# Attention followed by an MLP: more layer-norm rows transposed by transfers, token rows loaded one head earlier

## The chip, the cores and the metric

The kernel runs on one core of one Trainium2 chip. The metric is device time in microseconds: the median of several executions. Five engines work side by side: TensorE (PE: matmuls and its own transposes), VectorE (DVE), ScalarE (ACT), GpSimd (POOL) and SyncE (SP), which only issues transfers here. Each engine runs its instructions in the order in which the program issues them; waits between engines go through semaphores.

## The reference

For 8 batches of 8 heads, 576 tokens and head width 64, causal attention with a bias from a running sum of `s`, then a layer norm and a two-matrix MLP with a residual:

```python
scores = (q @ k.T) / 8                        # per batch and head, 576 x 576
cum    = cumsum(max(s, 0))                    # along the tokens
scores = where(causal, -1e9, scores + min(-(cum[:, None] - cum[None, :]), 0))
attn   = softmax(scores) @ v                  # 576 x 64
x      = heads side by side                   # 576 x 512 per batch
xn     = (x - mean) / sqrt(var + 1e-6) * g_ln
out    = x + max(xn @ w_ch1, 0) @ w_ch2       # 512 -> 2048 -> 512
```

## The kernel before

**Heads and units.** The 64 (batch, head) pairs are numbered n = 8b + h. The first batch and a half are written out step by step (`PLAN`); from n = 18 on a loop issues, for each n: `pre(n)`, the scores of head n, MLP units, `post(n)`, more units, and the attention-times-v of head n - 2 (`pv_next`). A *unit* is a quarter of an MLP tile: four 512-column matmuls on PE, either of the first matrix (`mlp1`, line 537, tile `ph`) or of the second (`mlp2`, line 555, tile `py`). A batch has 32 units in `queue`, and they fill PE between the attention steps. Line 983 sets the head (`end`) by whose close one batch's units are used up and the next batch's are queued: n = 19 for batch 0's, then 8i + 3 for i up to `NXD` = 6 and 8i + 4 above. `nu` is the number of units still given to a head after two fixed ones.

**Keys and queries.** Four heads make a group `gam` (16 groups, two a batch). Groups 0 to 4 are brought in by other means. From group 5 on, token rows are loaded in float32 by SP (`ld_rows`, line 175, tile `rowtmp`, five tiles of at most 128 tokens, two transfers each, a pool of six buffers), cast to bf16 by POOL into `rows[t]` with the bias columns beside them (`cast_rows`, lines 192 and 195), and transposed into `kq[home(gam)]` by a transposing transfer that SP issues (`tr_rows`, line 208). `rows` lies in the storage of `kq[2]`, which group 2 has used before; there is one `rows[t]` for each t, so a cast waits until the group before has been transposed, and two `kq` homes alternate. With m = n - 4 gam, `pre` loads tiles 0 and 1 at m = -6, 2 and 3 at -5, 4 at -4; `post` casts them one head later each, and transposes 0 and 1 at m = -4 and the rest at -3. The scores of the group start at m = 0. At n = 14 `pre` clears the unused columns of `rows` (line 855).

**Layer norm.** When a batch's attention is complete, DVE makes the normalised tiles `xn` (`ln_xn`, line 499): four tiles for an even batch, five for an odd one (the fifth holds the last 64 tokens of two batches). Each must be transposed into `xT` (or `xTm`) before `mlp1` reads it. Up to `NXD` the loop has PE transpose it (`ln_tr`, line 526, four 128 x 128 transposes a tile) and DVE or ACT copy it out of PSUM (line 116); for the last two batches SP issues a transposing transfer instead (`ln_tr_dma`, line 518). In the loop at batch b it is batch b - 1's rows that are normalised, at h = 1; the PE transposes follow at h = 2 and 3. In the transfer branch tiles 0 to 2 are normalised and sent at h = 1 and tiles 3 and 4 at h = 2, with a unit after each.

**What shares a queue.** SP issues, in program order: the row loads, the row transposes, the `xn` transfers and the stores of `out`. POOL issues the loads of v, of the weights and of the first pairs, and also runs the casts and the causal masking of the exponentials (`affine_select`, lines 366 and 396).

Of the kernel before, what the change touches and what calls it, by code (L numbers as in the profile page):

```python
# [9 lines left out]
F32 = mybir.dt.float32  # L10
# [5 lines left out]
P = 128  # L16
# [3 lines left out]
def kernel(  # L20
# [11 lines left out]
    nc = tc.nc  # L32
    B, H, S, D = q.shape
# [5 lines left out]
    NF = S // P  # L39
    NT = NF + 1  # L40
    TL = S - NF * P
    SP = NT * P
    BH = B * H
    KA = D + 4
    OB, OC, OD = 512, 1024, 1536
    EW = 1664
    G = 4
    NG = BH // G
    NPE = 5
    NM = 10  # L50
    NHW = 16
    NXD = 6
    KT = 96
    QT = 6
    QP = S // QT
# [31 lines left out]
    kq = [const.tile([P, 2, G, SP], BF16, name=f"kq{i}") for i in range(3)]  # L87


    def home(gam):  # L90
        return 2 if gam == 2 else gam % 2


    spare = kq[2].rearrange("p u h s -> p (u h s)")
    rows = [
        spare[:, i * 2 * G * P : (i + 1) * 2 * G * P].rearrange(
            "p (u h c) -> p u h c", u=2, h=G
        )
        for i in range(NT)
    ]  # L100
# [58 lines left out]
    def ld_cast_pair(g):  # L159
        ld_cast("k", g)  # L160
        ld_cast("q", g)

    def ld_cast_v(b, t):
        pn = P if t < NF else TL
        nc.gpsimd.dma_start(  # L165
            out=v_bf[b % 2][:pn, t, :, 0:D],
            in_=v[b, :, t * P : t * P + pn, :].rearrange("h s d -> s h d"),
        )

    def ld_rows(gam, t):  # L170
        pn = P if t < NF else TL
        b, h0 = gam // 2, (gam % 2) * G
        tmp = stage.tile([P, 2, G, D], F32, name="rowtmp", tag="st")
        for u, src in enumerate((k, q)):
            nc.sync.dma_start(  # L175
                out=tmp[0:pn, u],
                in_=src[b, h0 : h0 + G, t * P : t * P + pn, :].rearrange("h s d -> s h d"),
            )
        loaded["rows", gam, t] = tmp

    def ld_cast_rows(gam, t):
        pn = P if t < NF else TL
        b, h0 = gam // 2, (gam % 2) * G
        for u, src in enumerate((k, q)):
            nc.gpsimd.dma_start(
                out=rows[t][0:pn, u, :, 0:D],
                in_=src[b, h0 : h0 + G, t * P : t * P + pn, :].rearrange("h s d -> s h d"),
            )
# [10 lines left out]
    def bias_of_rows(gam, t):  # L199
        pn = P if t < NF else TL  # L200
        nc.vector.tensor_copy(
            out=rows[t][0:pn, :, :, D:KA], in_=cT[0:pn, t, :, gam * G : (gam + 1) * G, :]
        )

    def tr_rows(gam, t):
        pn = P if t < NF else TL
        o = t * 2 * G * P
        nc.sync.dma_start_transpose(  # L208
            out=kq[home(gam)]
            .rearrange("p u h s -> p (u h s)")[:, o : o + 2 * G * pn]  # L210
            .rearrange("p (h s) -> p h s", s=pn),
            in_=rows[t][0:pn].rearrange("p u h c -> p (u h c)"),
        )

    w1_r = moe_w_ch1.rearrange("(kd p) dh -> p kd dh", p=P)
# [2 lines left out]
    def ld_w1(c):  # L218
        sl = slice(c * 512, (c + 1) * 512)
        nc.gpsimd.dma_start(out=w1_bf[:, :, sl], in_=w1_r[:, :, sl])  # L220

    def ld_w2(i):
        nc.gpsimd.dma_start(
            out=w2_bf[:, 4 * i : 4 * i + 4, :], in_=w2_r[:, 4 * i : 4 * i + 4, :]
        )
# [3 lines left out]
    def aug(gam, eng, h0=0):  # L229
        r = slice(gam * G + h0, gam * G + G)  # L230
        i = home(gam)
        eng.dma_start(out=kq[i][D : D + 1, 1, h0:G, 0:S], in_=c_hi[r, :])
        for j in range(3):
            eng.dma_start(out=kq[i][D + 1 + j : D + 2 + j, 0, h0:G, 0:S], in_=c3[r, j, :])
# [214 lines left out]
    def x_tiles(b):  # L449
        ts_ = [xb[b][:, t, :] for t in range(NF)]  # L450
        if b % 2 == 1:
            ts_.append(xm[b // 2])
        return ts_
# [20 lines left out]
    def ln_rstd(b):  # L474
        n = len(x_tiles(b))
        rs = rstd[:, b, 0:n]
        nc.vector.tensor_scalar_add(out=rs, in0=mvs[b][:, 0:n, 1], scalar1=1e-6)  # L477
        nc.gpsimd.tensor_tensor(out=rs, in0=rs, in1=mhalf[:, 0:n], op=ALU.pow)  # L478

    def ln_aggr(b, t):  # L480
        nc.vector.bn_aggr(out=mvs[b][:, t, :], in_=st[b][:, t, 0 : 2 if b == 0 else 3, :])

    def ln_xn(b, t):
        tiles = x_tiles(b)
        if t >= len(tiles):
            return
        if b == 0:
            nc.vector.tensor_scalar(
                out=mean0[:, t : t + 1],
                in0=sum0[:, t, 0:1],  # L490
                scalar1=sum0[:, t, 1:2],
                scalar2=1.0 / Dm,
                op0=ALU.add,
                op1=ALU.mult,
            )
        else:
            ln_aggr(b, t)
        xn = xnp.tile([P, Dm], BF16, name="xn", tag="xn")
        nc.vector.scalar_tensor_tensor(  # L499
            out=xn,  # L500
            in0=tiles[t],
            scalar=mvs[b][:, t, 0:1] if b > 0 else mean0[:, t : t + 1],
            in1=gb,
            op0=ALU.subtract,
            op1=ALU.mult,
        )
        xns[b, t] = xn
        if b > 0 and t == len(tiles) - 1:
            ln_rstd(b)
# [86 lines left out]
    def run_units(n, dve_first=False):  # L596
        for i in range(n):
            if queue:
                first_unit[0] = dve_first and i == 0
                queue.pop(0)()  # L600
# [27 lines left out]
    nc.vector.memset(v_bf[0][0:TL, NF, :, D : D + 1], 1.0)  # L628
    for i in range(2):
        nc.vector.memset(kq[i][0:KA, 0, :, S:SP], 0.0)  # L630
    nc.vector.memset(kq[2][0:KA, 0, :, S:SP], 0.0)
    nc.vector.memset(eight, 1.0 / scale)
    nc.vector.memset(mhalf, -0.5)
    nc.vector.memset(c3[BH:KT], 0.0)
# [5 lines left out]
        in_=maskT,  # L640
# [16 lines left out]
    ld_cast_tile("q", NF)  # L657
    ld_cast_v(0, NF)

    for u, two in ((0, -1.0058441162109375), (1, 1.0019378662109375)):  # L660
        nc.gpsimd.memset(kq[2][D:KA, u].bitcast(F32)[:, :, 0 : S // 2], two)
    ld_w1(1)
    nc.gpsimd.memset(v_bf[1][:, 0:NF, :, D : D + 1], 1.0)
    nc.gpsimd.memset(v_bf[1][0:TL, NF, :, D : D + 1], 1.0)
# [185 lines left out]


    def pre(n):
        if n == 14:
            for r in rows:
                nc.gpsimd.memset(r[:, :, :, KA:P], 0.0)
        if n in PAIR_LOADS:
            ld_cast_pair(PAIR_LOADS[n])
        if n in (11, 12):
            ld_w2(n - 9)
        if n in (8, 9):  # L860
            aug(n - 5, nc.sync)
        for gam in range(NPE, NG):
            m = n - 4 * gam
            ts_ = {-6: (0, 1), -5: (2, 3), -4: (4,)}.get(m, ())
            for t in ts_:
                if gam < NHW:
                    ld_rows(gam, t)
                else:
                    ld_cast_rows(gam, t)
                    bias_of_rows(gam, t)  # L870
            if gam >= NHW:
                for t in {-4: (0, 1), -3: (2, 3, 4)}.get(m, ()):
                    tr_rows(gam, t)
        for nb in range(2, B):
            t = n - H * nb + (5 if nb == 2 else 6)
            if 0 <= t < NT:
                ld_cast_v(nb, t)

    def post(n):
        for gam in range(NPE, NHW):  # L880
            m = n - 4 * gam
            for t in {-4: (0, 1), -3: (2, 3)}.get(m, ()):
                tr_rows(gam, t)
            for t in {-5: (0, 1), -4: (2, 3), -3: (4,)}.get(m, ()):
                cast_rows(gam, t)
            if m == -3:
                tr_rows(gam, 4)

    def pv_next():
        pb, ph_ = pend.pop(0)  # L890
# [88 lines left out]
    for n in range(2 * H + 2, BH):  # L979
        b, h = n // H, n % H  # L980
        pre(n)

        end = next(m for m in [8 * i + (3 if i <= NXD else 4) for i in range(2, B)] + [BH + 3] if m >= n)
        nu = -(-len(queue) // (end - n + 1)) - 2
        scores(b, h)
        run_units(1, True)
        if h % 2 == 0:
            scores_d(b, h // 2)
        post(n)
        run_units(1)  # L990
        pv_next()
        pend.append((b, h))
        if b <= NXD:
            if n == 2 * H + 2:
                for t in range(3, NT):
                    ln_xn(1, t)
            if b > 2 and h == 1:
                for t in range(NT):
                    ln_xn(b - 1, t)
            for t in {2: (0, 1), 3: (2, 3, 4)}.get(h, ()):  # L1000
                ln_tr(b - 1, t, "act" if b == 2 else "dve")
                if t != 1 and t != 4:
                    run_units(1)
                    nu -= 1
        elif h in (1, 2):
            for t in ((0, 1, 2), (3, 4))[h - 1]:
                ln_xn(b - 1, t)
                ln_tr_dma(b - 1, t)
                run_units(1)
                nu -= 1  # L1010
        run_units(nu)
        if n == end:
            run_units(len(queue))
            queue += batch_units(b - 1)
# [41 lines left out]
```

## Time and profile before

| | |
|---|---|
| median of 3 executions | 358.01 us (356.86 to 359.27) |
| the profiled execution's own time | 358.78 us |
| its span, first to last instruction | 357.1 us |
| TensorE clock granted | 1.00 |
| busy: PE, DVE, ACT, POOL | 349.3, 196.2, 185.5, 162.2 us |
| DMA moved | 49.73 MB, mean 139 GB/s |
| transposing transfers by SP | 55 of rows (line 208), 9 of `xn` (line 518) |

The profile comes from one execution. The span is the time from the first to the last instruction; some 1.7 us of the profiled execution lie around it. A PE that is "busy" need not be working at its peak, because matmuls are pipelined and a record runs on after the next matmul has started; the distance between the starts of neighbouring matmuls tells what one costs. In the timeline a row reads: start in us, duration in us, engine, line, operation, output <- input, how many were merged, and in brackets an idle time before it with what ended it. [...]

### The profile page before, as it was taken

The numbers are of one execution on the slowest core, as the hardware profiler recorded it, in microseconds if no ns is written. First come the engines' busy times: TensorE is split into PE (matmuls) and PEld (weight loads), VectorE is DVE, ScalarE is ACT, GpSimd is POOL, SyncE is SP. The second block draws the span as 40 slices with busy tenths as digits, with TensorE's granted clock in tenths as the row PEclk, the third lists the DMA queues.
The fourth block names the chain that finished last, engine by engine and source line by source line (L and its number), as shares of the span: only waits on it lengthen the run. The fifth ranks groups of instructions, "written<-read, shape, count | busy, mean of one in ns | idle before, by whom it ended". The sixth has DMA issues, their size and how long they took to land.

```text
span 357.1 us, 8417 instructions
## 1 busy us (share of the span) xinstructions
PE 349.3 (98%) x3154; PEld 198.9 (56%) x3154; DVE 196.2 (55%) x535; ACT 185.5 (52%) x359; POOL 162.2 (45%) x344
## 2 busy tenths in 40 slices
PE   8999999999899999999999999999999999999995
PEld 3899666555455555555565555555555544444444
DVE  7788888944376536844384539543764582113111
ACT  4899886577434763267336743475366403402500
POOL 9997669458436742582556452665341010000000
PEclk9999999999999999999999999999999999999999
DMA  9999999999979998699979974999740043011013
GB/s 151 170 180 171 199 190 166 191 192 168 184 147 204 153 212 149 106 226 172 171 129 213 207 145 84 222 180 174 158 119 2 0 80 113 0 61 60 0 32 89
DMA packets 169098, 49.73 MB, mean 139 GB/s; under 512 B 157744, under 2 KB 164448, under 8 KB 169056
## 3 DMA queue, kind: packets, MB, share of 16 engines
q1 hardware_dynamic: 116016, 36.53, 53.6%
q0 software_dynamic: 51600, 11.87, 37.1%
q10 hardware_dynamic: 1440, 0.79, 0.8%
q8 instruction: 25, 0.41, 0.5%
q14 instruction: 17, 0.14, 0.1%
HBM read 37.11 MB, written 9.44 MB: 130 GB/s over the span
## 4 chain that ended last, share of the span: by engine, by line
PE 84%; DVE 6%; DMA 3%; SPq 3%; POOL 2%; issue 1%; ACT 1%; DVEq 0%; POOLq 0%; ACTq 0%
PE py L555 31%; PE ph L537 29%; PE pot L424 6%; PE sc L346 3%; PE sb L346 3%; PE sa L346 3%; PE ph L817 2%; DVE xn L499 2%; DMA kq<-kq 2%; PE st L715 2%; SPq L175 1%; DMA rowtmp<-in_q_dram 1%; PE trx L526 1%; SPq L208 1%; PE pot L773 1%
## 5 line engine op out<-in xcount | busy, mean ns | idle before, releaser
L555 PE MATMUL py<-w_bf,hT 128*128 128x512 bf16 (+1 forms) x592 | 135.5, 373 | 0.4 <-DVE yo L564 0.4
L537 PE MATMUL ph<-xT,w_bf 128*128 128x512 bf16 x480 | 114.0, 379 | 0.0
L547 ACT ACTIVATE hT<-ph 128x512 bf16<-128x512 f32 x101 | 60.2, 597 | 74.3 <-PE ph L537 74.3
L555 PEld LDWEIGHTS <-hT 128*128 128x128 bf16 x592 | 53.7, 98 | 50.7 <-issue 0.9
L537 PEld LDWEIGHTS <-w_bf 128*128 128x128 bf16 x544 | 48.7, 97 | 50.5 <-issue 3.1
L366 POOL TENSOR_SCALAR_AFFINE_SELECT er<-er 128x256 bf16<-128x256 bf16 x108 | 43.7, 419 | 53.2 <-ACT er L357 52.3
L357 ACT ACTIVATE er<-sa 128x512 bf16<-128x512 f32 x56 | 33.3, 595 | 64.9 <-PE sa L346 50.3
L545 DVE TENSOR_SCALAR hT<-ph 128x512 bf16<-128x512 f32 x35 | 24.2, 692 | 57.3 <-PE ph L537 52.4
L192 POOL CAST kq<-rowtmp 128x512 bf16<-128x512 f32 (+1 forms) x55 | 33.5, 609 | 29.3 <-DMA rowtmp<-in_q_dram 27.4
L346 PEld LDWEIGHTS <-kq 68*128 68x128 bf16 x412 | 29.7, 97 | 23.5 <-DMA kq<-kq 2.0
L424 PEld LDWEIGHTS <-er 128*128 128x128 bf16 x840 | 32.8, 98 | 11.9
L436 DVE RECIPROCAL rinv<-pot 128x5 f32<-128x5 f32 x56 | 10.7, 192 | 50.0 <-PE pot L424 49.8
L564 DVE SCALAR_TENSOR_TENSOR yo<-py,rstd,xb 128x512 f32<-128x512 f32 x32 | 24.0, 749 | 24.2 <-PE py L555 19.5
L424 PE MATMUL pot<-v_bf,er 128*128 128x65 bf16 x840 | 34.7, 194 | 0.0
L165 POOL DMA_DIRECT2D v_bf<-in_v_dram x40 | 34.4, 867 | 0.3 <-DVE kq L116 0.3
L357 ACT ACTIVATE er<-sb 128x512 bf16<-128x512 f32 x56 | 33.5, 598 | 1.3 <-PE sb L346 1.3
L357 ACT ACTIVATE er<-sc 128x512 bf16<-128x512 f32 x56 | 34.1, 610 | 0.0
L478 POOL TENSOR_TENSOR rstd<-rstd,mhalf 128x4 f32<-128x4 f32 (+1 forms) x8 | 8.9, 1115 | 45.0 <-DVE rstd L477 45.0
L438 DVE TENSOR_TENSOR xb<-pot,rinv 128x256 f32<-128x256 f32 x56 | 23.8, 424 | 1.9
L346 PE MATMUL sb<-kq 68*128 68x64 bf16 (+1 forms) x156 | 21.4, 241 | 1.7 <-DMA kq<-kq 1.7
L462 DVE BATCH_NORM_STATS2 stats<-xb 128x6 f32<-128x128 f32 (+1 forms) x84 | 21.9, 320 | 0.3
L346 PE MATMUL sc<-kq 68*128 68x256 bf16 (+1 forms) x200 | 21.7, 226 | 0.1
(116 smaller groups left out, 354.2 us busy)
## 6 DMA issues: line engine op xcount, KB each, us to landing
out_dram<-yo SPq DMA_DIRECT2D x32, 256.0 KB
rowtmp<-in_k_dram SPq DMA_DIRECT2D x44, 128.0 KB
rowtmp<-in_q_dram SPq DMA_DIRECT2D x44, 128.0 KB
v_bf<-in_v_dram POOLq DMA_DIRECT2D x32, 128.0 KB, 6.1
w_bf<-in_moe_w_ch_dram POOLq DMA_DIRECT2D x8, 512.0 KB, 9.1
kq<-kq SPq DMA_TRANSPOSE x55
kp<-in_k_dram POOLq DMA_DIRECT2D x6, 144.0 KB, 8.7
qp<-in_q_dram POOLq DMA_DIRECT2D x6, 144.0 KB, 8.8
```

The source lines that it names most:

```text
L165: nc.gpsimd.dma_start(out=v_bf[b % 2][:pn, t, :, 0:D], in_=v[b, :, t * P : t * P + pn, :].rearrange("h s d -> s h d"),)
L192: nc.gpsimd.tensor_copy(out=rows[t][0:pn, :, :, 0:D], in_=loaded.pop(("rows", gam, t))[0:pn])
L346: nc.tensor.matmul(a[:, c + a0 - q0 : c + a1 - q0], lhsT=k_cols(b, h, kb), rhs=cols, start=True, stop=not (pe_mask and diag),)
L357: nc.scalar.activation(out=e[:, o : o + 512], in_=a, func=ACT.Exp, scale=scale)
L366: nc.gpsimd.affine_select(out=two, in_=two, compare_op=ALU.is_ge, fill=0.0, base=0, pattern=[[0, 2], [1, P]], channel_multiplier=-1,)
L424: nc.tensor.matmul(pot[:, t, :], lhsT=e[:, o : o + P], rhs=vv[:, kb, h, :], start=(kb == 0), stop=(kb == last),)
L438: nc.vector.tensor_tensor(out=xb[b][:, :, hs], in0=pot[:, 0:NF, 0:D], in1=rinv[:, 0:NF].unsqueeze(2).to_broadcast([P, NF, D]), op=ALU.mult,)
L537: nc.tensor.matmul(ph, lhsT=w1_bf[:, kd, fb * P : (fb + 1) * P], rhs=xT[:, kd, :], start=(kd == 0), stop=(kd == KD - 1),)
L545: nc.vector.tensor_scalar_max(out=hT[:, fb, :], in0=ph, scalar1=0.0)
L547: nc.scalar.activation(out=hT[:, fb, :], in_=ph, func=ACT.Relu)
L555: nc.tensor.matmul(py[t], lhsT=hT[:, fb, t * P : (t + 1) * P], rhs=w2_bf[:, fb, c0:c1], start=(fb == 0), stop=(fb == FB - 1),)
L564: nc.vector.scalar_tensor_tensor(out=yo, in0=py[t], scalar=rs, in1=x[:, c0:c1], op0=ALU.mult, op1=ALU.add)
```

## The change

`NXD` goes from 6 to 2. So the rows of batches 2 to 5 take the transfer branch, with its placing at h = 1 and h = 2, and the `end` of batches 1 to 4's units moves from n = 8i + 3 to 8i + 4 for i = 3 to 6. Groups above 5 load their token rows one head earlier (m = -7, -6, -5); casts stay where they were. The row transposes of a group become three: tiles 0 and 1 together at m = -4, tiles 2 and 3 together and tile 4 alone at m = -3. The clearing of `rows` at n = 14 goes; in its place the early clearing of `kq[2]` covers all partitions that the rows use, and one part of it moves from DVE to POOL. The last part of the diff is in a branch that, with `NXD` = 2, is only entered at b = 2.

```diff
-    NXD = 6
+    NXD = 2
...
-    def tr_rows(gam, t):
-        pn = P if t < NF else TL
-        o = t * 2 * G * P
+    def tr_rows(gam, t0, t1):
+        pn = P if t0 < NF else TL
+        o, n = t0 * 2 * G * P, (t1 - t0) * 2 * G
         nc.sync.dma_start_transpose(
             out=kq[home(gam)]
-            .rearrange("p u h s -> p (u h s)")[:, o : o + 2 * G * pn]
+            .rearrange("p u h s -> p (u h s)")[:, o : o + n * pn]
             .rearrange("p (h s) -> p h s", s=pn),
-            in_=rows[t][0:pn].rearrange("p u h c -> p (u h c)"),
+            in_=spare[0:pn, o : o + n * P],
         )
...
-    nc.vector.memset(kq[2][0:KA, 0, :, S:SP], 0.0)
...
+    nc.gpsimd.memset(kq[2][:, :, :, S:SP], 0.0)
     for u, two in ((0, -1.0058441162109375), (1, 1.0019378662109375)):
-        nc.gpsimd.memset(kq[2][D:KA, u].bitcast(F32)[:, :, 0 : S // 2], two)
+        nc.gpsimd.memset(kq[2][D:P, u].bitcast(F32)[:, :, 0 : S // 2], two)
...
-        if n == 14:
-            for r in rows:
-                nc.gpsimd.memset(r[:, :, :, KA:P], 0.0)
...
-            ts_ = {-6: (0, 1), -5: (2, 3), -4: (4,)}.get(m, ())
+            ts_ = {-6: (0, 1), -5: (2, 3), -4: (4,)}.get(m + 1 * (gam > NPE), ())
...
-            for t in {-4: (0, 1), -3: (2, 3)}.get(m, ()):
-                tr_rows(gam, t)
+            if m == -4:
+                tr_rows(gam, 0, 2)
+            elif m == -3:
+                tr_rows(gam, 2, NF)
             for t in {-5: (0, 1), -4: (2, 3), -3: (4,)}.get(m, ()):
                 cast_rows(gam, t)
             if m == -3:
-                tr_rows(gam, 4)
+                tr_rows(gam, NF, NT)
...
-            if b > 2 and h == 1:
-                for t in range(NT):
-                    ln_xn(b - 1, t)
+            for t in {1: (0, 1, 2), 2: (3, 4)}.get(h, ()) if b > 2 else ():
+                ln_xn(b - 1, t)
+                if t in (1, 2, 4):
+                    run_units(1)
+                    nu -= 1
             for t in {2: (0, 1), 3: (2, 3, 4)}.get(h, ()):
                 ln_tr(b - 1, t, "act" if b == 2 else "dve")
-                if t != 1 and t != 4:
+                if t not in (1, 4) and nu > 0:
                     run_units(1)
                     nu -= 1
```

More of the change, by code (lines that the diff above doesn't have):

```diff
@@ L870, in pre @@
                     bias_of_rows(gam, t)
-            if gam >= NHW:
-                for t in {-4: (0, 1), -3: (2, 3, 4)}.get(m, ()):
-                    tr_rows(gam, t)
         for nb in range(2, B):
@@ L881, in post @@
             m = n - 4 * gam
-            for t in {-4: (0, 1), -3: (2, 3)}.get(m, ()):
-                tr_rows(gam, t)
+            if m == -4:
+                tr_rows(gam, 0, 2)
+            elif m == -3:
+                tr_rows(gam, 2, NF)
             for t in {-5: (0, 1), -4: (2, 3), -3: (4,)}.get(m, ()):
```

## The prediction

> **What bounds the kernel now.** I read the page first: busy times, and the chain that ended last.
>
> ```profile
> PE 349.3 (98%) x3154; PEld 198.9 (56%) x3154; DVE 196.2 (55%) x535; ACT 185.5 (52%) x359; POOL 162.2 (45%) x344
> PE 84%; DVE 6%; DMA 3%; SPq 3%; POOL 2%; issue 1%; ACT 1%; DVEq 0%; POOLq 0%; ACTq 0%
> ```
>
> PE has work in 349.3 of 357.1 us and carries 84% of the chain. So time comes off in two ways only: fewer matmuls, or fewer of the gaps. The PE timeline of a head with row transposes (n = 34 and 35) shows both.
>
> ```profile
> 142.27 0.62 PE L424 MATMUL pot<-v_bf,er 128*128 128x65 bf16 x15
> 142.72 0.39 PE L526 MATMUL trx<-ident,xn 128*128 128x128 bf16 x4
> 142.95 1.03 PE L555 MATMUL py<-w_bf,hT 128*128 128x512 bf16 x4
> 143.81 0.39 PE L526 MATMUL trx<-ident,xn 128*128 128x128 bf16 x4
> 144.03 1.03 PE L555 MATMUL py<-w_bf,hT 128*128 128x512 bf16 x4
> ...
> 145.94 1.89 PE L555 MATMUL py<-w_bf,hT 128*128 128x512 bf16 x8 [0.21 <-DVE yo L564]
> ```
>
> A tile's four transposes push the next matmul back by 142.95 - 142.72 = 0.23 us and 144.03 - 143.81 = 0.22 us. The last row is a gap: `py` waits for DVE, which is working through five `xn` in a row.
>
> The longest gap in PE is elsewhere, at n = 24, the first head of group 6:
>
> ```profile
> 91.00 0.38 PE L346 MATMUL sa<-kq 68*128 68x512 bf16 x1
> 93.08 0.39 PE L346 MATMUL sb<-kq 68*128 68x64 bf16 x3 [1.71 <-DMA kq<-kq]
> ```
>
> In other heads `sb` starts 0.22 us after `sa`, here 2.08: 1.86 us are lost. SP's timeline shows why the transpose is late.
>
> ```profile
> 59.25 5.19 SPq L208 DMA_TRANSPOSE kq<-kq  x2
> 64.55 0.99 SPq L582 DMA_DIRECT2D out_dram<-yo  x2
> 65.70 5.45 SPq L208 DMA_TRANSPOSE kq<-kq  x3
> 71.21 0.57 SPq L175 DMA_DIRECT2D rowtmp<-in_k_dram  x1
> ...
> 80.92 7.34 SPq L208 DMA_TRANSPOSE kq<-kq  x5
> ```
>
> Group 6's first row load stands behind all of group 5's transposes and goes out at 71.21; the casts wait for it, and the last transpose goes out at 86.96 and lands at 93.03.
>
> Last, the load on the transfer engines by stage (the last two columns are busy share and GB/s):
>
> ```profile
> 60.00:65.00 5.00, 5.00 (x44) 2.78 (x43) 4.54 (x15) 3.57 (x7) 4.58 (x12) 1.00 1.81 119
> 65.00:70.00 5.00, 5.00 (x47) 2.92 (x46) 4.83 (x11) 3.37 (x9) 1.43 (x3) 1.00 1.48 213
> 142.00:146.00 4.00, 3.79 (x43) 2.37 (x41) 3.85 (x10) 0.64 (x3) 0.81 (x1) 1.00 0.00 0
> 291.50:292.50 1.00, 1.00 (x7) 0.45 (x5) 0.96 (x3) 0.00 (x0) 0.00 (x0) 1.00 0.67 131
> ```
>
> They are crowded up to 70 us and have holes later: 4 us at 142, 2 us at 105.
>
> **PE transposes removed.** Batches 2 and 4 have 4 tiles, 3 and 5 have 5: 18 tiles x 0.22 us = 4.0 us of PE. All of it lies on the path, between matmuls that follow back to back. DVE also loses 18 copies of 0.41 us, worth nothing, since it has 160 us idle.
>
> **DVE gap.** The head that starts at 144.90 takes until 150.52, 5.62 us; a plain one takes 4.58 and three transposed tiles 0.66, so 0.38 us are the gap. The same stands at 220.95 to 226.57. With three `xn` at h = 1, a unit between each, and two at h = 2, a `yo` stands behind one or two `xn` (about 1 us each with the aggregate), not five: both gaps go, 0.75 us. Bounds: 0 to 0.75.
>
> **Transfers added.** 18 transposing transfers of `xn`. The trace has this operation in batch 6:
>
> ```profile
> 255.23 2.51 SPq L518 DMA_TRANSPOSE xT<-xn  x2
> 257.84 0.54 SPq L582 DMA_DIRECT2D out_dram<-yo  x1
> 258.47 4.29 SPq L518 DMA_TRANSPOSE xT<-xn  x2
> ```
>
> About 1.2 us of SP each, and by the completion records 2.4 to 3.7 us until they land. There the row loads are over; a row transpose among them landed in 2.8 to 7.9 us (median 4.3), which I take for the new ones: 4.5, at most 8. The last `xn` goes out at the end of head 8b + 2 and `mlp1` reads it from head 8b + 5. For batches 3 to 5 the two heads between hold 4 and 3 units: 4.6 + 3.7 us, and 0.66 for the scores, 9 us: covered even at 8. For batch 2 one period has nine heads, and by line 984 the heads get 4, 4, 4, 4, 4, 5, 4, 2, 1 units: heads 27 and 28 take 2.9 and 2.0 us, so the cover is 5.5 us. Cost: 0 to 2.5 us once, I take 0.2, nearest to the median landing. The same 2-and-1 pattern stands in the trace before (heads 59 and 60, `sa` at 259.69, 262.55, 264.59), without a PE gap. The total number of units, and the tail, stay.
>
> Their load: the window at 291.5 holds one such transfer's worth (131 GB/s for 1 us = 131 KB) at a share of 0.67. 18 x 0.67 = 12 us of all engines over some 150 us, five tiles a batch = 3.4 us in 37, next to holes like those at 105 and 142, just where the new transfers fall. So no price, but with the holes filled a late transfer has less slack.
>
> [...]
>
> **Row transposes merged.** 55 transfers become 33, for the same bytes. SP's issue was 1.29 us (median) for 1024 columns and 1.22 for 512, so 2048 columns lie between 1.3 and 2.6. SP's sum goes from 55 x 1.29 = 71 us to 33 x (1.3 to 2.6) + 18 x 1.22 = 65 to 108, over 190 us: it fits. Tile 0 now waits for tile 1's cast, 0.8 us on POOL, with three heads in hand.
>
> **Loads a head sooner.** From group 7 on this only adds slack: before, POOL waited 27.4 us in all for `rowtmp`. At h = 1 and 2 SP waits for each `xn` on DVE; behind it stand the stores and the next head's loads, which are needed two heads later. For group 6 it moves the loads of tiles 0 and 1 ahead of group 5's second and third transposes. So the last transpose of group 6 can go out when its casts are done, at about 81 rather than 86.96, and lands before 91: the 1.86 us go.
>
> What is late next is group 5. Before, its last transpose landed at 72.76, and head 20's `sb` came at 72.81, 0.26 after `sa`: on time by nothing. Now four row loads are ahead of it in the queue. In this trace loads in a run land 0.6 us apart, so 4 x 0.6 = 2.4 us later. Against it stands the removed clearing, 2.25 us of POOL at 53.95, just ahead of group 5's first cast at 58.46: its first transposes can start up to 2 us earlier, but into a stage with a share of 1.8, so I count 0.9 of it. New gap at n = 20: 1.5 us; bounds 0 (POOL's gain counts in full) and 3.5 (it counts nothing and the stores slip in too).
>
> **Clearing moved.** One memset of 0.17 us leaves DVE in its unbroken start: 0.1 us gained. POOL's added one, some 0.5 us, delays the bias rows of group 2 (issued 17.91), first read at 28.4: hidden, else 0.5.
>
> **Sum** against the profiled execution (span 357.1, own time 358.78): -4.0 - 0.75 - 1.86 - 0.1 + 1.5 + 0.2 = -5.0. Span 352.1, own time 353.8. The profiled run lies 0.8 above the median, within the runs' 2.4 spread, so I subtract from the median: 358.01 - 5.0 = 353.0.
>
> **Rivals.**
> 1. *Group 5 is not late* (the freed POOL time counts in full): -4.0 - 0.75 - 1.86 - 0.1 = -6.7, 351.3. For it: the first casts do wait for POOL. Against: the shares of 1.81 and 1.48.
> 2. *A wait takes the gain's place*: the four loads and crowded queue hold group 5 for the full 3.5, group 6 slips with it (1.86 stays), batch 2's last `xn` costs 2.5: -4.85 + 3.5 + 2.5 = +1.2 at the worst, 354.5 to 359.2.
> 3. *Slower: the transfer engines fill up*. Shares above 1 may already be full. If `xT` lands more than 9 us after issue, PE waits at the first `mlp1` of all four batches. At 12 us it is 4 x 3, and batch 2's shorter cover adds 3.5: +15.5 - 6.7 + 1.5 = +10, 368. It passes zero at about 9.5 us. Against: nothing in the loop landed later than 7.9.
> 4. *The merged transfers don't save*: SP takes 2.6 us or more each, and the loads behind them lose their head. Then 1.86 stays: -3.1, 354.9.
>
> **How the numbers follow.** Chances: forecast (351.9 to 354.4) 0.43, rival 1 0.25, rival 2 0.16, rival 3 0.09, rival 4 0.07. Range: 350.3 to 356.5; it leaves out about half of rival 2, rival 3, and a little below. One per cent, about what a measurement of this kernel can tell from no change, is 3.6 us. Faster by more (under 354.4): forecast, rival 1, a part of 4: 0.72. Within: most of 2, the rest of 4: 0.18. Slower: 0.10.
>
> **What the next profile would show.** L526 with 36 matmuls instead of 108; L518 with 27 transfers; L208 with 33; `sb` at n = 24 right behind `sa`; at n = 20 a wait of `sa` or `sb` for `kq` near 72 us, the term I am least sure of. Plain heads should keep 4.58 us, and heads 26, 27, 34 and 35 come down to it. Waits of `ph` L537 for `xT` at heads 29, 37, 45 or 53 would make me wrong, as would waits for `kq` every fourth head.

## The result and the profile after

The changed kernel took **372.84 us** (median; 371.74 to 373.98) against 358.32 us (356.86 to 359.27) beside it: 1.041 times the time of before, 95% interval 1.036 to 1.046. It is slower by 14.5 us, where I had forecast 5 us less. The profiled execution took 373.98 us, with a span of 372.3. Here and below a median takes in every execution of a kernel, while a ratio leaves out the few that were over 1.5 per cent slower than its fastest.

The page of the changed kernel, engines and the chain that ended last:

```profile
PE 350.2 (94%) x3082; PEld 195.6 (53%) x3082; DVE 190.1 (51%) x516; ACT 186.3 (50%) x359; POOL 161.2 (43%) x340
PE 61%; DMA 19%; POOL 8%; DVE 5%; SPq 3%; issue 3%; ACT 0%; POOLq 0%; DVEq 0%; ACTq 0%
```

PE has 72 matmuls less and is busy for 94% of the span instead of 98; in the chain DMA has 19% where it had 3. The waits of PE in the changed kernel (total, times, longest) name the places:

```profile
PE ph L537 <- DMA xT<-xn: 7.7, 3, 5.1
PE sa L346 <- DMA kq<-kq: 4.0, 3, 2.6
PE sb L346 <- DMA kq<-kq: 2.3, 2, 1.5
...
PE ph L537 <- DVE yo L564: 1.1, 1, 1.1
PE py L555 <- DMA w_bf<-in_moe_w_ch_dram: 0.7, 1, 0.7
```

The 1.1 put down to `yo` is at head 53, where `xT`'s last tile landed at 241.84 and `ph` started at 241.93: it is a fourth wait for `xT`. So PE waits at the first `mlp1` of each of the four batches, and for `kq` at heads 20, 40, 48 and 56. At head 20 both waits are long:

```profile
76.26 0.38 PE L346 MATMUL sa<-kq 68*128 68x512 bf16 x1 [2.63 <-DMA kq<-kq]
78.13 0.38 PE L346 MATMUL sb<-kq 68*128 68x64 bf16 x3 [1.49 <-DMA kq<-kq]
```

The wait at head 24 is gone, as forecast: `sb` stands right behind `sa` in PE's timeline of the changed kernel.

```profile
97.99 0.38 PE L346 MATMUL sa<-kq 68*128 68x512 bf16 x1
98.21 0.38 PE L346 MATMUL sb<-kq 68*128 68x64 bf16 x3
```

The largest new wait, at head 29, in the same timeline (in brackets the idle time ahead and what ended it), with the eight matmuls behind it and the next eight:

```profile
123.50 3.28 PE L537 MATMUL ph<-xT,w_bf 128*128 128x512 bf16 x8 [5.09 <-DMA xT<-xn]
...
127.07 1.89 PE L537 MATMUL ph<-xT,w_bf 128*128 128x512 bf16 x8
```

Eight matmuls take 3.28 us behind the wait and 1.89 later: PE's clock had been halved. The table by windows shows it, here for 77 to 81 us (behind head 20's wait) and 124 to 127 us (behind head 29's); the last three numbers are the granted clock, the mean busy share of the transfer engines and GB/s. Taken alone, 79 to 81 us and 124 to 126 us have a granted clock of 0.50.

```profile
77.00:81.00 4.00, 2.87 (x15) 1.35 (x15) 0.49 (x1) 1.69 (x4) 1.15 (x4) 0.69 1.31 219
124.00:127.00 3.00, 3.00 (x21) 1.25 (x20) 0.69 (x1) 0.19 (x1) 2.79 (x6) 0.61 1.03 187
```

**The account.** The two profiled executions differ by 15.2 us. With the start of every head's first `sa` from both traces, the 14.5 us up to head 63 can be added up (the other 0.7 come behind it):

| stage | before | after | difference |
|---|---|---|---|
| up to `sa` of head 20 | 72.54 | 76.26 | +3.7: wait for `kq` 2.6, for `w_bf` 0.7 |
| head 20 | 4.67 | 7.95 | +3.3: `sb` waits 1.5, the rest half clock |
| heads 21 to 24 | 20.29 | 18.41 | -1.9: the old wait at head 24 |
| heads 25 to 28 | 19.32 | 14.97 | -4.35: 0.9 for the transposes, 3.45 only moved (last row but one) |
| head 29 | 4.58 | 11.21 | +6.6: wait 5.1, half clock 1.5 |
| heads 30 to 56 | 128.21 | 131.83 | +3.6: 7.5 of waits, less 3.9 for transposes and DVE gaps |
| heads 57 to 62 | 25.90 | 29.35 | +3.45: the heads with 2 units and 1 moved from here to 27 and 28 |
| sum | | | +14.5 |

The 7.5 and the 3.9 are each measured by themselves: how much longer than plain heads (4.57 and 4.63) those with waits are in the changed kernel, and those with transposes or DVE gaps in the kernel before. What I had counted as gain came in full: 0.9 + 3.9 = 4.8 us for transposes and DVE gaps (I had 4.75) and 1.9 at head 24. About 21 us of new waits and half clock came on top.

Where the last `xn` of batch 2 was meanwhile is seen in SP's timeline of the changed kernel. DVE had this `xn` ready at 113.1, and head 29 wanted `xT` at 118.2.

```profile
106.74 4.79 SPq L208 DMA_TRANSPOSE kq<-kq  x2
111.62 3.52 SPq L518 DMA_TRANSPOSE xT<-xn  x2
115.23 0.54 SPq L582 DMA_DIRECT2D out_dram<-yo  x1
115.86 1.27 SPq L518 DMA_TRANSPOSE xT<-xn  x1
117.18 0.57 SPq L175 DMA_DIRECT2D rowtmp<-in_k_dram  x1
117.81 0.50 SPq L175 DMA_DIRECT2D rowtmp<-in_q_dram  x1
118.35 0.51 SPq L175 DMA_DIRECT2D rowtmp<-in_k_dram  x1
118.90 0.51 SPq L175 DMA_DIRECT2D rowtmp<-in_q_dram  x1
119.50 1.19 SPq L518 DMA_TRANSPOSE xT<-xn  x1
```

From 106.74 on SP does nothing but issue. Two row transposes hold it for 4.8 us, so the first `xn` transfer, ready at 108.1, goes out at 111.6; the last one stands behind four row loads, goes out at 119.50, 6.4 us after it was ready, and lands 3.9 us later. The transfer itself isn't late; its turn is. SP's DMA instructions that start between 100 and 250 us take 139.2 us (row transposes 61.5, row loads 45.1, `xn` 24.2, stores 8.4), 136.5 of them inside these 150 us; before it was 118.3 (58.3, 48.6, none, 11.3).

### The profile page after: what moved, and what is told of

Same layout as the page of the kernel before. It is cut to its first block, busy times and chain, and to the rows that moved or that the text cites. A ratio compares the mean times of both kernels' runs of the same rounds, so it can differ in the third digit from the quotient of the medians.

```text
span 372.3 us, 8265 instructions
## 1 busy us (share of the span) xinstructions
PE 350.2 (94%) x3082; PEld 195.6 (53%) x3082; DVE 190.1 (51%) x516; ACT 186.3 (50%) x359; POOL 161.2 (43%) x340
## 3 DMA queue, kind: packets, MB, share of 16 engines
q1 hardware_dynamic: 125104, 38.89, 59.2%
## 4 chain that ended last, share of the span: by engine, by line
PE 61%; DMA 19%; POOL 8%; DVE 5%; SPq 3%; issue 3%; ACT 0%; POOLq 0%; DVEq 0%; ACTq 0%
PE ph L537 26%; PE py L555 25%; DMA kq<-kq 5%; PE pot L424 4%; DMA xT<-xn 4%; DMA w_bf<-in_moe_w_ch_dram 4%; DMA kp<-in_k_dram 3%; PE sb L346 2%; SPq L175 2%; DMA v_bf<-in_v_dram 2%; PE sc L346 2%; PE sa L346 2%; DMA rowtmp<-in_q_dram 2%; POOL rowb L153 2%; DVE xn L499 2%
## 5 line engine op out<-in xcount | busy, mean ns | idle before, releaser
L537 PE MATMUL ph<-xT,w_bf 128*128 128x512 bf16 x480 | 117.1, 386 | 8.8 <-DMA xT<-xn 7.7
L366 POOL TENSOR_SCALAR_AFFINE_SELECT er<-er 128x256 bf16<-128x256 bf16 x108 | 45.0, 424 | 97.4 <-ACT er L357 96.3
L537 PEld LDWEIGHTS <-w_bf 128*128 128x128 bf16 x544 | 49.3, 99 | 61.5 <-issue 12.3
L545 DVE TENSOR_SCALAR hT<-ph 128x512 bf16<-128x512 f32 x35 | 24.2, 692 | 72.4 <-PE ph L537 67.5
L436 DVE RECIPROCAL rinv<-pot 128x5 f32<-128x5 f32 x56 | 10.7, 192 | 59.9 <-PE pot L424 59.7
L424 PEld LDWEIGHTS <-er 128*128 128x128 bf16 x840 | 32.8, 98 | 12.2 <-issue 0.5
L346 PE MATMUL sa<-kq 68*128 68x512 bf16 x56 | 21.3, 381 | 4.0 <-DMA kq<-kq 4.0
```

Source lines behind the costliest of these rows:

```text
L346: nc.tensor.matmul(a[:, c + a0 - q0 : c + a1 - q0], lhsT=k_cols(b, h, kb), rhs=cols, start=True, stop=not (pe_mask and diag),)
L366: nc.gpsimd.affine_select(out=two, in_=two, compare_op=ALU.is_ge, fill=0.0, base=0, pattern=[[0, 2], [1, P]], channel_multiplier=-1,)
L424: nc.tensor.matmul(pot[:, t, :], lhsT=e[:, o : o + P], rhs=vv[:, kb, h, :], start=(kb == 0), stop=(kb == last),)
L537: nc.tensor.matmul(ph, lhsT=w1_bf[:, kd, fb * P : (fb + 1) * P], rhs=xT[:, kd, :], start=(kd == 0), stop=(kd == KD - 1),)
L545: nc.vector.tensor_scalar_max(out=hT[:, fb, :], in0=ph, scalar1=0.0)
```

## The experiments

Theory S, formed from this: SP's queue is full, and what stands late in it is late for PE (its first form, which blamed the early loads and the merged transposes, is called theory Q in the expectations of r1 to r8). Theory T, my rival 3: the transfer engines are full. Each run is told with its time and its ratio to the kernel before on the same chip.

### Which part costs it

```diff
 # r1: before, with one edit
-    NXD = 6
+    NXD = 2
 # r2: the change, with NXD = 6 again
 # r3: the change, with the row loads at their old heads
-            ts_ = {-6: (0, 1), -5: (2, 3), -4: (4,)}.get(m + 1 * (gam > NPE), ())
+            ts_ = {-6: (0, 1), -5: (2, 3), -4: (4,)}.get(m, ())
 # r4: the change, with tr_rows(gam, t) for one tile again
 # r15: the change, with the clearing in its old places
+        if n == 14:
+            for r in rows:
+                nc.gpsimd.memset(r[:, :, :, KA:P], 0.0)
```

> The kernel before with only the xn rows of batches 2 to 5 moved to SP's transfers (NXD = 2); row loads, row transposes and clearing as before. Theory Q (SP's order: the new waits come from what stands ahead in SP's in-order queue, row loads moved ahead of row transposes and merged transposes that hold SP 2.7 us and more): without those two edits little stands ahead, 354 to 359 us. Theory T (the transfer engines are full, the 18 added transfers themselves push everything late): the waits of ph for xT and of sa and sb for kq past 100 us stay, only the wait at head 20 goes; 364 to 368 us.

> The change without its xn part: row loads a head sooner, row transposes merged, clearing moved, PE transposes of xn as before. Theory Q: head 20 waits as in the changed kernel (4.4 us and slow matmuls after it) and some of the waits of heads 40, 48 and 56 stay, head 24's wait goes: 360 to 364 us. Theory T: the load is that of before, so 356 to 360 us.

> The change without the earlier loads: xn by transfers, transposes merged, clearing moved. Theory Q: head 20 is on time again (6 us back), the four loads no longer stand ahead of the transposes, head 24's wait comes back (1.9): 358 to 364 us. Theory T: same bytes in the loop, 368 to 372 us.

> The change without the merging: xn by transfers, loads a head sooner, five transposes a group, clearing moved. Theory Q: SP is held for less at a time (1.3 us against 2.7), xn transfers go out earlier: 360 to 367 us. Theory T: same bytes, 370 to 374 us.

> The change without the moved clearing alone (the 2.25 us of POOL stay at head 14, the small memset on DVE). I had counted 0.9 us for the clearing at head 20: by that, group 5's casts start later and the waits for kq at head 20 grow by about 1 us, 374. Rival: the clearing's place is worth nothing or less, since with it the casts and loads ahead of head 17 come closer together and w_bf is late there (a wait of 0.7 to 1.8 us in the nine profiles of kernels with the clearing moved, and in one of the four without): that wait goes, 372 to 373. The waits for xT at heads 29, 37, 45 and 53 stay under both.

| kernel | median us | ratio, 95% interval |
|---|---|---|
| the change | 372.84 | 1.041 (1.036 to 1.046) |
| r1, `xn` by transfer alone | 364.25 | 1.019 (1.014 to 1.023) |
| r2, all but that | 362.12 | 1.011 (1.006 to 1.016) |
| r3, all but the early loads | 363.81 | 1.017 (1.013 to 1.021) |
| r4, all but the merging | 372.30 | 1.041 (1.035 to 1.047) |
| r15, all but the clearing's move | 370.02 | 1.031 (1.026 to 1.035) |

The `xn` transfers are slower by themselves, the rest is slower by itself, and together they cost about 1 per cent more than the sum. By the ranges that I had expected, r1 and r4 spoke for T, r2 and r3 for Q: neither held as first put. The early loads, which I had counted as slack, cost 2.4 per cent, some 9 us, beside the `xn` transfers; in the profiles about half of it lies ahead of head 25. Merging costs and saves nothing: SP is held for 3.3 us (median of 22) by a transpose of two tiles and was held 1.3 by one of a single tile.

The `xn` transfers alone (r1), PE's waits:

```profile
PE sa L346 <- DMA kq<-kq: 2.9, 1, 2.9
PE ph L537 <- DMA xT<-xn: 2.8, 1, 2.8
PE sa L346 <- issue: 2.4, 1, 2.4
```

They are at heads 40, 29 and 56. Behind the ones at heads 29 and 40 are stretches of half clock, 6.8 and 3.4 us long. All but `xn` (r2) waits at head 20 (2.0 and 0.3) and for `w_bf` (0.7).

**The clearing** has the other sign than I gave it: undone, it saves about 1 per cent (r15). In POOL's timeline these are group 5's first and last casts, of the kernel before:

```profile
58.46 0.62 POOL L192 CAST kq<-rowtmp 128x512 bf16<-128x512 f32 x1
...
62.99 0.60 POOL L192 CAST kq<-rowtmp 64x512 bf16<-64x512 f32 x1
```

and of the change, with the fourth between them:

```profile
56.38 0.62 POOL L192 CAST kq<-rowtmp 128x512 bf16<-128x512 f32 x1
...
61.32 0.62 POOL L192 CAST kq<-rowtmp 128x512 bf16<-128x512 f32 x1 [1.08 <-DMA rowtmp<-in_q_dram]
...
63.02 0.60 POOL L192 CAST kq<-rowtmp 64x512 bf16<-64x512 f32 x1 [0.21 <-DMA rowtmp<-in_q_dram]
```

The first cast comes 2.08 us sooner, the last one not at all, since the fourth and the last now wait for their row loads (1.08 and 0.21). Head 20 began between 72.3 and 74.8 us in the seven profiles with the clearing in its old place (before, r1, r8, r11, r15, r16, r18), and between 74.9 and 76.8 in the eleven with it moved (r9 and r10, where ScalarE issues the loads, left out; r12, r14, r17 and r18 have two units fewer ahead of head 20). The ranges all but touch, and r8, which is the kernel before up to head 25, began head 20 some 2.3 us later than the kernel before did. A wait for `w_bf` of 0.7 to 1.8 us near 60 us is in all eleven, but also in r8 and r16, where the clearing is kept. SP's timeline shows more. This is group 5's first transpose (tiles 0 and 1) in the change, and then in r15:

```profile
57.88 4.47 SPq L208 DMA_TRANSPOSE kq<-kq  x1
```

```profile
59.95 1.45 SPq L208 DMA_TRANSPOSE kq<-kq  x1
```

In the ten profiles with the clearing moved and the transposes merged it goes out at 57.7 to 59.2, holds SP for 4.0 to 4.7 us and lands 10.5 to 12.2 us after its issue, at 69.2 to 71.4. In r15 and r18 it goes out at 59.9, holds SP for 1.5 and 1.6 us and lands after 7.5 and 7.7, at 67.4 and 67.6. So what was sent sooner landed later; why it took longer is not settled.

### Full transfer engines, or SP

```diff
 # r7: the change; xn transfers of batches 2 to 5 carry 128 of 512 columns (the short tile all)
+            k = KD if b > 5 or t == NF else 1
+            nc.sync.dma_start_transpose(out=xT_dst(b, t)[:, 0:k], in_=xn[:, 0 : k * P])
 # r8: before, with 18 more loads that nobody reads
+        nc.scalar.dma_start(out=spill[...], in_=q[0, 0:G, 0:P, :]...)    # 128 KB
 # r11: before, with the 18 xn transfers into a spare buffer, PE transposing as before
+                    nc.sync.dma_start_transpose(out=spill[...], in_=xns[b - 1, t])
 # r9: the change, r10: before, with the row loads issued by ScalarE
-            nc.sync.dma_start(
+            nc.scalar.dma_start(
                 out=tmp[0:pn, u],
```

> The changed kernel, but the xn transfers of batches 2 to 5 (tiles 0 to 3) carry 128 of 512 columns, and the first MLP matmul of these batches reads that quarter four times; so this part of the output is left wrong. Same number, order and waits of transfers, 1.6 MB fewer. Theory Q: order is the same, 369 to 373 us. Theory T: three quarters of the added load are gone, 358 to 364 us.

> The kernel before with 18 added row loads of 128 KB (512 packets of 256 bytes, like an xn transfer) into unused memory, issued by ScalarE in the heads where the change issues its xn transfers; nothing reads them. SP's queue and all waits as before. Theory Q: no row of the kernel waits on them, 357 to 360 us. Theory T: the added load alone pushes the row transposes late, 363 to 368 us.

> The kernel before, with PE transposing xn as before, and 18 added transposing transfers of the same xn tiles by SP into unused memory, placed as the change places them; nothing reads them. Theory S: SP's queue is as full as after the change, so the row transposes of groups 10, 12 and 14 come late: 360 to 365 us, with waits for kq at heads 40, 48 and 56. Rival theory C (only the readers of xT make the wait, the row pipeline is not touched): 357 to 359 us.

> The changed kernel with its 110 row loads issued by ScalarE's queue in place of SP's; all else as changed, same bytes. Theory S (SP's own issue time: its DMA instructions took 118 us of the 150 between 100 and 250 us before, and 139 after, so anything it waits for makes all behind it late): SP falls to some 95 of 150, the waits for xT and kq go, 352 to 358 us, if ScalarE bears some 0.5 us an issue. Theory X (transposing transfers get in each other's way in flight, whoever issues the rest): the waits stay, 365 to 372 us.

> The kernel before with its 110 row loads issued by ScalarE's queue. Theory S: SP has room, head 24's wait (1.9 us) goes if ScalarE's issue time costs nothing: 355 to 358 us. Theory X: 356 to 359 us. Tells what the move of the loads costs or gains by itself.

**r7**: 369.05 us, 1.027 (1.019 to 1.034). In it the first layer of batches 2 to 5 reads the 128 columns four times, so their output isn't the reference's; the number of matmuls is the same. With a quarter of the bytes, 5.6 us of wait are left at head 29, and 3.9 and 1.1 for `kq`. **r8**: 358.40 us, 0.999 (0.996 to 1.002): 2.3 MB more in the same heads cost nothing. So theory T falls as the main cause; a part, some 1.4 per cent of the time, goes with the bytes.

**r11**: 359.79 us, 1.005 (1.002 to 1.009). SP is as full as in the change (137 of 150 us), with all the transfers and nobody waiting for them, and the profiled execution (357.97, one of the two quickest of ten) has no wait of PE for `kq`, not even the one at head 24. So theory S has to be narrowed: a full queue by itself costs half a per cent. The landings tell why so little. The last row transposes for heads 40, 48 and 56 land 0.3 and 0.4 us after and 0.1 ahead of the head's first `sa` in r11, and 1.8, 4.0 and 2.9 ahead of it in the kernel before: the full queue makes them 2.1 to 4.4 us later, and in r11 the slack just takes it. Two things are different in the change: PE reads the transferred `xT` at the first `mlp1`, and it is quicker by the 0.9 or 1.5 us a batch that its own transposes took, so it wants `kq` sooner as well. (Theory X, in the expectations of r9 and r10, is a rival in which transposing transfers slow each other in flight. In r1 the row transposes land after 4.6 us in the median, before after 4.3: too little for it.)

**r9**: 402.04 us, 1.111 (1.101 to 1.120); **r10**: 374.91 us, 1.047 (1.041 to 1.054). SP falls to 81 of 150 us in r9, and the waits for `kq` go and those for `xT` shrink to 1.1, as S says. But ScalarE, with the loads in its own queue, brings its `hT` late; PE's waits in r9 begin with

```profile
PE ph L537 <- ACT hT L547: 25.2, 6, 6.2
```

so the time says nothing on S. The other way to empty SP, `xn` transfers from another queue than the row transposes, was not tried.

### The order in the queue, and PE's cover

```diff
 # r5 (shortened): the change; from head 17 on row loads are issued behind the head's row transposes
-        for gam in range(NPE, NG): ... ld_rows(gam, t)         # in pre
+        if n >= 4 * NPE - 3:                                   # at the end of post
+            for gam in range(NPE, NG):
+                ld_group(gam, n)                       # the row loads due at head n
 # r6: as r5, and each batch's units a head later
-        end = next(m for m in [8 * i + (3 if i <= NXD else 4) ...
+        end = next(m for m in [8 * i + (3 if i <= NXD else 5) ...
 # r12: as r5, and periods of eight heads only
+        end = next(m for m in [8 * i + 4 ...
 # r14: as r12, with NXD = 3 (batch 2 transposed by PE again)
 # r17: as r12, and the row loads behind the xn transfers too (at the head's end)
 # r18: as r17, with the clearing in its old places
 # r13: as r5, with NXD = 6;  r16: before, with the early loads in r5's order alone
```

> The changed kernel with one edit: from head 17 on, a head's row loads are issued behind its row transposes, no longer ahead of them. Same transfers, same bytes. Theory Q (what stands ahead in SP's queue makes the waits): the waits for kq at heads 20, 40, 48 and 56 go, those for xT at heads 29, 37, 45 and 53 stay in part; 358 to 364 us. Theory T (the transfer engines are full): 369 to 374 us.

> As the run with the loads behind the transposes, and each batch's MLP units start one head later (8i + 5 in place of 8i + 4), so an xn transfer has 4.6 us more. Same transfers and bytes. Theory Q: nothing is late any more, 351 to 356 us, faster than both kernels. Theory T: what is late by load stays late; the xT waits turn into kq waits, 363 to 370 us.

> All of the change, the row loads behind the row transposes (as in the fifth run), and every period of units ends at head 8i + 4, so that none has nine heads and heads 27 and 28 no longer get 2 units and 1. Theory of the cover (what costs most is that PE comes too early at the first mlp1 of batch 2): heads 27 and 28 take about 4.2 us each where they took 2.9 and 2.0, so the wait at head 29 falls from 4.8 to about 1.4 us, and a stretch of half clock of 3.4 us (1.7 lost) goes with it: 5 us less than the fifth run, 362 to 363, or +4 on the kernel before. Rival (SP's queue is late by what it holds, and only moves): the wait comes back at other heads and the time stays near 368.

> The change without the transfers of xn (batches 2 to 5 transposed by PE as before), and with the row loads behind the row transposes. Theory of the order: group 5 is not late at head 20, group 6 is not late at head 24 (1.86 us), so 356 to 356.5, or 0.994 of before. Rival (the loads or the merged transfers cost something by themselves): like the second run, 361 to 362, with a wait for kq at head 20.

> As the kernel with even periods, but batch 2's xn transposed by PE again (transfers for batches 3 to 5 alone). Theory of the cover: no wait at head 29 at all; waits of about 0.7 and 1.9 us at two of heads 37, 45 and 53 at most, a stretch of half clock at most; 14 tiles x 0.22 = 3.1 us and 1.86 us gained: 355 to 358, 0.99 to 1.0. Rival (the queue is late in every batch): the 5 us wait moves to head 37, 362 to 364.

> Before with one edit: row loads a head sooner from group 6 on, but issued behind the row transposes of their head. Theory of the order: the wait of 1.71 us at head 24 goes, group 5 at head 20 is as on time as before, and nothing else waits: 356.2, 0.995 of before. Rival (a gain of this size is given back to waits for kq at head 20, as in the thirteenth run): 358, 1.00.

> The kernel with even periods, with one more step of the same kind: from head 17 on a head's row loads are issued behind its xn transfers too, at the head's end. Theory of SP's order: four row loads of 0.5 to 0.6 us no longer stand ahead of the last xn transfer of a batch (in the kernel with even periods it went out at 115.12, with the loads from 112.78 on), so it goes out some 2.3 us sooner, and the waits for xT of 1.5 to 1.8 us at heads 29, 37, 45 and 53 go: 4.5 us less, 361, or 1.01 of before. Rival (the landing, not the place in the queue, sets the waits): they stay, 365.8.

> As the run beside it, with the clearing left in its old place as well. Undone from the whole change, the clearing gave 2.8 us back. If that comes from the stage up to head 20 by itself, 358 here, level with before, and no wait for kq at head 20; if it came from that kernel's other waits, 361 as in the run beside it.

**r5**: 367.85 us, 1.025 (1.019 to 1.031), between the two ranges expected. The same transfers in another order: all four places with waits for `kq` are gone, and head 29's wait stays (4.8; all for `xT` in the next fence, in PE's waits of r5):

```profile
PE ph L537 <- DMA xT<-xn: 7.5, 3, 4.8
```

**r6**: 365.94 us, 1.019 (1.014 to 1.025), where S had 351 to 356. A head more of cover leaves one wait for `xT`, of 3.3 us, now at head 30; four waits for `yo` (3.2 in all) are new, because a `yo` now stands behind DVE's row statistics.

**r12**: 365.80 us, 1.023 (1.017 to 1.029). With 4 and 3 units in heads 27 and 28, in place of 2 and 1, the wait at head 29 falls from 4.8 to 1.6 (1.4 expected) and no half clock follows in the profile. So two thirds of that wait were the short cover of batch 2. But waits of 1.6, 1.3 and 1.5 us stay at heads 29, 37 and 45, and the total gains 2 us, not 5; the intervals of r5 and r12 overlap.

**r14**: 362.62 us, 1.012 (1.007 to 1.017), where 355 to 358 were expected. No wait at head 29, and from head 25 to 57 it is ahead of before, 150.34 against 152.10 us with 128 units in each: three batches' 3.9 us, less 2.1 of waits. This is the one place where the transfers paid. But head 25 came 2.3 us late, and with four units (3.45 us) fewer ahead of it, since the periods of units end a head later; these units are done from head 57 on. So 5.7 us were lost up to head 25. There the profile has waits for `kq` at head 20 (1.6), for `w_bf` (1.2) and for `qp` (1.0), and a stretch of half clock behind head 20's (1.7).

**r17**: 367.21 us, 1.025 (1.021 to 1.029), where 361 were expected. The mechanism worked: the last `xn` of batch 2 goes out at 113.19 instead of 115.12, and none of r12's three waits for `xT` is left. The gain did not come, since the row loads, now last, bring `kq` late at heads 32, 40 and 56 (5.3 us of the 6.3 below; head 20 waits as it did in r12). PE's waits of r12, and then of r17:

```profile
PE ph L537 <- DMA xT<-xn: 2.8, 2, 1.5
...
PE sa L346 <- DMA kq<-kq: 1.5, 2, 0.8
```

```profile
PE sa L346 <- DMA kq<-kq: 4.7, 3, 2.3
PE sb L346 <- DMA kq<-kq: 1.6, 3, 0.8
```

(In r12 a third wait, of 1.6 us at head 29, is put down to "issue"; the last `xT` tile landed at 119.05 and `ph` started at 119.14, so it is one for `xT`.) This pair is the clearest sign of what the queue does: its order decides who waits, `xT` or `kq`; as long as everything stays in it, somebody does.

**r18**: 363.68 us (359.38 to 365.27), 1.018 (1.013 to 1.022): the clearing kept gives 3.5 us, as it gave 2.8 in r15 (though the intervals of r17 and r18 overlap a little), and head 20 waits for nothing; of the 358 that I expected for that case only the quickest execution, the profiled one, came near.

**r13**: 359.40 us, 1.004 (1.001 to 1.007); **r16**: 357.03 us, 0.998 (0.996 to 1.000). Without the `xn` transfers, the early loads behind the transposes do take away the wait at head 24. In r13 it is given back at head 20 (0.9), where its rival had a wait, and to `w_bf` (1.2), though 361 to 362 did not come; in r16 some 1 us of 1.86 is left, less than can be told from no change. No version here beats the kernel before by more.

## Why the prediction was wrong

- **Right: the terms of the gain.** 4.75 us for transposes and DVE gaps, measured 4.8; 1.86 at head 24, measured 1.9; the counts at L526 (36), L518 (27) and L208 (33), and the end of the `yo` gaps. The landing of the new transfers too: 2.5 to 7.0 us, median 3.8, for "4.5, at most 8". "So no price" for their load is right in the main: loads of the same size cost nothing in r8, though by r7 some 1.4 per cent goes with the bytes.
- **Wrong, the step that failed: "The last `xn` goes out at the end of head 8b + 2".** I took the place in the program for the time of issue. In batch 2 head 26 ended at 112.70 and the transfer went out at 119.50; in batches 3 to 5 the last one that `mlp1` wants went out 4.5 to 5.1 us after that head's end. Cover of 5.5 and 9 us was reckoned from the wrong start. I had "0 to 2.5 us once"; it was 5.1, 1.6, 1.0 and 1.1 us at four places, and half clock.
- **Wrong, and the reason for it: SP's sum, "65 to 108, over 190 us: it fits".** It holds only the transposes. The 110 row loads, at 0.5 to 0.6 us each, and the stores are in the same queue; with them SP is at 136.5 of 150 us. And a transpose of two full tiles, at 3.3 us, lies past my upper end of 2.6. It was to be had from the view of SP's timeline that I showed.
- **Wrong: "From group 7 on this only adds slack".** POOL's slack, yes; but in SP's queue the early loads stand ahead of the transposes and the `xn` transfers that are due first. Undone it gives some 9 us (r3), 5.1 of them from head 25 to 57 in the profiles, and by order alone the waits for `kq` go (r5).
- **Mis-sized: head 20.** I had 1.5 us (0 to 3.5); 2.6 + 1.5 of waiting came, and half clock. The 0.9 us that I counted for POOL are not there: the last cast is as late as before, group 5's first transpose goes out sooner but takes 11.5 us to land, and r15 shows the clearing's move as a loss, as r18 does less clearly.
- **The rivals.** Rival 3 gave the nearest time (368) by luck, for a reason that fell: no `xn` transfer took more than 7.0 us to land, against its 9. Rival 4's premise held (a merged transfer of two tiles held SP for 3.3 us in the median, for over 2.6 in 17 of 22) without its effect. The sign I had wrong because no rival had the `xn` transfers late by what stands ahead of them in SP's queue. By themselves the transfers made the kernel 1.9 per cent slower (r1). In the change they took no longer to land than I had reckoned (2.5 to 7.0 us, for at most 8), and went out late (the last one of batch 2 6.4 us after it was ready).
- **Open.** In r1, with the same transfers on SP as in r11, the full queue costs much. How much of that is PE's quicker pace, which takes the slack that r11 lived on, and how much the new readers, no run separates. Why group 5's first transpose takes longer to land when the clearing is moved is open too.

## What to carry to other kernels

When work moves to a queue, add up everything that this queue issues in the stage, plain loads and stores as well, and write down for each new instruction what stands ahead of it at the moment it becomes ready: its time of issue comes from there, not from its place in the program (119.50 us in place of 112.70 for batch 2's last `xn`). SP's queue went from 79% to 91%, and in no order tried here did both readers go without a wait: moving one kind of transfer back made the other late. And an engine that is freed of work reaches its next input sooner, so the cover of every transfer shrinks by what was gained (worked out, not measured by itself).

## What was not expected of the hardware

- **Half clock after short gaps.** From one matmul's start to the next, PE lost its full clock (the granted one was 0.50 in the changed kernel's two stretches) behind gaps of 5.0 us (r5, for 6.83 us), but also of 2.15 (r5, for 3.41 us), of 1.86 (r14, head 20, for 3.41 us) and of 1.80 (r3, head 29, for 3.41 us), while nothing followed gaps of 2.09 (before, head 24), 2.18 (r2, head 20) and 2.77 us (r1, head 56). At half clock a stretch of 3.41 us costs 1.7 (worked out from the 0.50), if PE has work all through it. So a wait of 2 us may cost 2 or nearly 4. The length of the gap alone does not tell which: behind the one of 1.80 us, 1.61 of it idle, half clock came, behind those of 2.18 and 2.77 it did not.
- **ScalarE as an issuer of loads.** Moving 110 row loads from SP to ScalarE cost the kernel before 17 us (r10), though ScalarE is busy for 52% of its span.
- **Transfers that nobody waits for were nearly free**: 18 loads of 128 KB issued by ScalarE (r8) changed nothing that could be measured (0.999, 0.996 to 1.002), 18 transposes issued by SP (r11) cost half a per cent (1.005, 1.002 to 1.009).
